# Two splits of 600 rows as 352 and 248, another table for block 0, and an expert's row numbers made tile by tile

## The chip, the cores and the metric
The program runs on one core of one Trainium2 chip. The metric is the device time of one execution in microseconds (us); a kernel's time is the median of several executions. TensorE (PE) does the matmuls and, beside them, the weight loads (PEld); VectorE (DVE) and ScalarE (ACT) do the elementwise work; GpSimd (POOL) issues the indirect transfers (gathers and scatters); SyncE (SP) issues the other transfers.

## The reference
A chunked attention feeds a dense layer pair with a hard-swish, and that feeds a mixture of eight experts with two chosen for each row. Cut to what is computed:

```python
# attention: q, k, v (4, 8, 576, 64), chunks of 64 rows, each chunk for itself
scores = q_c @ k_c.T / sqrt(64); attn = softmax(scores); x = (attn @ v_c)     # -> x (2304, 512)
# dense pair, w_in (512, 2048), w_out (2048, 512)
h = x @ w_in
x = (h * clip(h + 3, 0, 6) / 6) @ w_out
# experts: E = 8, w1 (8, 512, 1024), w2 (8, 1024, 512)
noisy = x @ w_gate + log1p(exp(x @ w_noise)) * noise
top2, top2_w = two largest of noisy per row, softmax over the two
for e in range(8):
    rows = those that chose e
    out[rows] += top2_w * (relu(x[rows] @ w1[e]) @ w2[e])
```

## The kernel before
**Precision.** Each float32 operand is split in a high and a low part, and a product is three matmul passes (high x high, high x low, low x high; `PASSES`). Weights come from memory as `raw` (SyncE, L165), ScalarE makes the high part (L171) and VectorE the low part (L172).

**Dense pair.** The 2304 rows go in five blocks of 4, 3, 4, 4 and 3 tiles of 128 rows. A unit is 128 of the 2048 inner columns: the first layer (`s1`, L346) gives a bank that ScalarE and VectorE turn into `g`, and the second layer (`s2`, L358) adds it to a sum per row tile. Block 0 runs beside the attention and beside the unpacking of the weights. Its order on TensorE, VectorE and ScalarE is written out by hand in the strings `FIRST` and `REST`: `s3.1` is unit 3's first layer, pass 1 (L391), `y3.1` its second layer (L416), `rl`, `rm`, `g`, `gl` the four steps from the one to the other (L397 to L409), `ca`, `cb`, `ct`, `wh`, `wl` the unpacking of a unit's weights (L194 to L220), `sc` to `xo` the steps of an attention tile. Blocks 1 to 4 follow.

**Routing.** The gate of a block is laid among the matmuls of the next work by `route`, in ticks: `tick()` is called after every three matmuls of `s2` and runs what is due. `gate_pos` (two small matmuls, L600 and L601) turns the choice into a place in each expert's list, a scatter writes row number and weight to a table in memory (L623), and `exp_slots` reads a part of that table back (SyncE, L634).

**Experts.** `groups` holds, in order, expert 0 in two parts of three and two tiles, experts 1 to 6 whole (five tiles, `CT`; 600 rows at most, `CAP`), and expert 7 in two parts. Each has eight units `u` of 128 inner columns. For a whole expert a unit begins with two first-layer parts of 300 columns each, 24 matmuls in all; its second layer is written transposed, each weight block with 352 (L741) and 248 (L745) columns. A group in parts has as many columns in a first-layer matmul as it has rows.

Experts 0 and 1 fetch their rows by one gather for a tile (`exp_gather`, L676), and TensorE transposes them. From expert 2 on, a tile is fetched as quarter rows by four gathers of 128 quarter rows (`exp_gather_q`, L659; the last tile has three), whose numbers `iq` VectorE makes from the row numbers `tq` (`exp_index`, L653). `tq` comes by one load from the table and three copies (SyncE, L645, L647). VectorE turns the quarters (`exp_tr_q`, L472), ScalarE and VectorE write the high and the low part (L671, L672). A fetched tile lies in one of three buffers (tag `x2`); `iq` and `tq` have one each.

What an expert's rows need is laid in the units of the groups before by `at(side, unit, function, ...)`. In the order of time: `gi == 1` is the second part of expert 0, `gi == 2` is expert 1, from about 527 to 588 us. TensorE, VectorE, ScalarE and SyncE run in the order in which the code is written; GpSimd's order is the scheduler's.

**The end.** In the last unit of the last group, `exp_last` adds the last three units to the two sums tile by tile (L721); `exp_y` scales each sum by the rows' weights and GpSimd scatter-adds it to the output (L799). The second tile's first half is scaled by VectorE (L790), its second half by ScalarE (L791).

Of the kernel before, what the change touches and what calls it, by code (L numbers as in the profile page):

```python
# [19 lines left out]
P = 128  # L20
# [17 lines left out]
def cols(t0, nt, cap=WIDE):  # L38
    return min(cap - t0 * P, nt * P)
# [10 lines left out]
sc0 warm7.4 mx0 sub0 e0 su0 sc1 ra0 mx1 rb0 sc2 nmx1 nm0 e1.0 mx2 pt0 sc3 e1.1 sub2 warm14.2 mx3 e2 ra1 nmx3  # L50
rb1 e3.1 nm1 su2 pt1 warm13.2 e3.0 ca0 ra2 cb0 at1 rb2 ct0 at0 xo1 ra3 nm2 wh0 xo0 rb3 ca2 pt2 hi0 nm3 at2
wl0 pt3 hi1 xo2 lo0 at3 s0.0.0 lo1 hi2 xo3 cb2 s0.1.0 hi3 lo2 s0.2.0 ct2 s0.0.1 lo3 wh2 s0.1.1 ca1 s0.2.1
wl2
# [3 lines left out]
ca6 wh3 rm1 s2.2 wl3 g1 cb6 y1.0 rl2 gl1 ct6 y1.1 rm2 wh6 y1.2 ca5 g2 wl6 sc4 ca8 cb5 s3.0 mx4 ct5 s3.1 nmx4  # L57
gl2 wh5 s3.2 e4.0 cb8 y2.0 wl5 e4.1 ca7 y2.1 ct8 ca10 wh8 y2.2 cb7 ra4 ct7 s4.0 cb10 wh7 s4.1 rl3 rb4 wl8
rm3 s4.2 wl7 g3 rl4 ca9 y3.0 gl3 ct10 y3.1 cb9 wh10 y3.2 rm4 wl10 g4 s5.0 nm4 s5.1 ct9 gl4 wh9 pt4 ca12 s5.2
at4 wl9 cb12 y4.0 ca11 ct12 y4.1 cb11 wh12 y4.2 ct11 wl12 wh11 xo4 rl5 wl11 sc5 hi4 rm5 s6.0 mx5 g5 lo4 s6.1  # L60
nmx5 gl5 e5.0 s6.2 ca14 cb14 y5.0 e5.1 ca13 ct14 y5.1 ra5 cb13 wh14 y5.2 rb5 ct13 s7.0 wl14 wh13 ca16 s7.1
rl6 cb16 rm6 s7.2 ct16 g6 rl7 y6.0 gl6 wh16 wl13 y6.1 wl16 rm7 y6.2 ca15 g7 s8.0 cb15 ca18 s8.1 ct15 gl7
wh15 s8.2 cb18 y7.0 ca17 wl15 y7.1 ct18 cb17 wh18 y7.2 ct17 s9.0 wl18 wh17 nm5 s9.1 wl17 pt5 ca20 rl8 s9.2
at5 rm8 cb20 g8 rl9 y8.0 gl8 ca19 y8.1 ct20 cb19 wh20 y8.2 ca22 ct19 xo5 cb22 wh19 sc6 hi5 wl20 s10.0 mx6
wl19 s10.1 nmx6 ct22 e6.1 s10.2 rm9 lo5 g9 wh22 ca21 y9.0 gl9 rl10 cb21 e6.0 y9.1 wl22 y9.2 ct21 rm10 wh21
s11.0 g10 wl21 s11.1 gl10 ca24 s11.2 ra6 cb24 y10.0 ca23 ct24 y10.1 cb23 wh24 ct23 y10.2 wl24 wh23 s12.0
ca26 wl23 s12.1 rl11 cb26 rm11 s12.2 ct26 g11 rl12 rb6 y11.0 gl11 wh26 ca25 y11.1 wl26 cb25 y11.2 ca28 ct25
s13.0 nm6 wh25 s13.1 rm12 wl25 g12 pt6 gl12 s13.2 at6 ca27 cb28 y12.0 ct28 y12.1 cb27 wh28 y12.2 ct27 wl28
wh27 xo6 wl27 s14.0 rl13 ca30 hi6 cb30 s14.1 rm13 ct30 s14.2 g13 lo6 wh30 y13.0 gl13 wl30 y13.1 rl14 ca29
y13.2 cb29 ct29 s15.0 rm14 wh29 s15.1 g14 wl29 gl14 s15.2 ca31 y14.0 cb31 ct31 y14.1 rl15 wh31 rm15 y14.2  # L70
wl31 g15 gl15
"""
EARLY = 384
# [7 lines left out]
def tile_kernel(ctx, tc, qkv, w1u, w2u, wg, noise, out):  # L81
# [269 lines left out]
    def s2(acc, g, w, tiles, first, last, passes=None):  # L351
# [32 lines left out]
    def first_s1(u, i, half=None):  # L384
        w, n = st["w", "m", u], BT[0] * P
        if ("h0", u) not in st:
            st["h0", u] = hbank(n) if u else pairs[0][:, :n]
        a, b = (((0, 0), (0, 1), (1, 0)) if u else ((0, 0), (1, 0), (0, 1)))[i]
        c = slice(0, n) if u else slice(half * n // 2, (half + 1) * n // 2)
        for kd in range(KD):  # L390
            nc.tensor.matmul(st["h0", u][:, c], w[:, a, kd * P:(kd + 1) * P], xb[0][:, b, kd, c],  # L391
                             start=(i == 0 and kd == 0), stop=(i == 2 and kd == KD - 1))

    def first_rl(u):
        h, r = st["h0", u], work.tile([P, DM], F32, tag="r", bufs=2, name="r")
        st["r0", u] = r
        nc.scalar.activation(r, h, AF.Relu, bias=b3)  # L397

    def first_rm(u):
        h, r = st["h0", u], st["r0", u]  # L400
        nc.vector.scalar_tensor_tensor(r, r, 6.0, h, op0=ALU.min, op1=ALU.mult)
# [855 lines left out]
```

## Time and profile before

| | |
|---|---|
| time, median of 3 executions | 925.06 us (924.91, 925.06, 928.58) |
| the profiled execution: its own time, and its span | 928.22 us, 926.3 us |
| mean granted clock of TensorE | 0.991 of full |
| TensorE busy | 902.0 us, 97% of the span |
| VectorE, ScalarE, GpSimd busy | 53%, 35%, 25% |

The profile is of one execution; its time stands a little above its span, which is the stretch that the records cover. Busy times are sums over the span. A matmul's end is modelled, so that the spacing of starts, or a row of the chain that ended last, tells more of its cost than its own length.

### The profile page before, as it was taken

What the parts mean: (1) busy time and instruction counts of PE and PEld (TensorE: products, weight loads), DVE (VectorE), ACT (ScalarE), POOL (GpSimd) and SP (SyncE); (2) the same over time, 40 slices, a digit from 0 to 9 for tenths busy, and PEclk for the clock granted to TensorE, in tenths of its full rate; (3) what the DMA queues carried; (4) which work ended last, traced back from release to release, by engine and by line L of the source; (5) the groups of instructions that cost most, each with busy time, mean ns of one, the idle gap of its engine ahead of it and who ended that gap; (6) DMA issues with size and microseconds to landing.
All of it is one profiled execution on the core that took longest, in us unless ns stands there. A gap on an engine that the chain in (4) does not pass through costs nothing.

```text
span 926.3 us, 15379 instructions
## 1 busy us (share of the span) xinstructions
PE 902.0 (97%) x6271; PEld 800.0 (86%) x6271; DVE 495.4 (53%) x950; ACT 321.7 (35%) x611; POOL 230.5 (25%) x212
## 2 busy tenths in 40 slices
PE   8999999999999999999999989899999999999996
PEld 5777788877788777888988889899999999999985
DVE  7999956535543553356542624454655565462321
ACT  5555433323332332245532512142342424332110
POOL 0000000030002000204015172448273645605051
PEclk9999999999999999999999998999999999999999
DMA  9736522122247400035433741277776848654462
GB/s 341 241 106 196 165 75 86 49 61 63 69 170 258 130 13 1 1 101 129 147 104 70 190 119 44 52 208 183 187 159 150 204 121 229 155 154 74 109 80 33
DMA packets 68993, 116.38 MB, mean 126 GB/s; under 512 B 17936, under 2 KB 38544, under 8 KB 68912
## 3 DMA queue, kind: packets, MB, share of 16 engines
q1 hardware_dynamic: 57552, 95.33, 33.8%
q0 software_dynamic: 11360, 19.98, 11.8%
q8 instruction: 51, 0.84, 0.4%
q14 instruction: 30, 0.25, 0.1%
HBM read 85.13 MB, written 30.09 MB: 124 GB/s over the span
## 4 chain that ended last, share of the span: by engine, by line
PE 88%; DVE 6%; DMA 2%; issue 1%; ACT 1%; POOL 0%; POOLq 0%; SPq 0%; ACTq 0%
PE bp L346 40%; PE bp L358 22%; PE bp L741 10%; PE bp L745 7%; PE bp L416 2%; DVE u L199 1%; PE bp L391 1%; DVE u L204 1%; PE pair L314 1%; DMA raw<-in_w1u_dram 1%; DVE w L220 1%; PE pair L232 1%; PE pair L293 1%; DMA lead<-in_qkv_dram 1%; DVE u L194 1%
## 5 line engine op out<-in xcount | busy, mean ns | idle before, releaser
L358 PE MATMUL bp<-w,g 128*128 128x512 f32 (+1 forms) x906 | 231.0, 398 | 0.1
L346 PE MATMUL bp<-Xa,w 128*128 128x300 f32 (+3 forms) x1152 | 195.0, 320 | 3.1 <-issue 2.8
L358 PEld LDWEIGHTS bp<-w,g 128*128 128x128 f32 (+1 forms) x906 | 165.6, 187 | 35.4 <-DVE g L435 1.0
L346 PEld LDWEIGHTS bp<-Xa,w 128*128 128x128 f32 x1152 | 173.3, 190 | 16.0 <-issue 6.1
L741 PE MATMUL bp<-g,w 128*128 128x352 f32 x576 | 162.2, 324 | 3.9 <-issue 3.9
L745 PE MATMUL bp<-g,w 128*128 128x248 f32 x564 | 155.7, 278 | 1.2 <-issue 1.2
L713 DVE SCALAR_TENSOR_TENSOR g<-bp,g 128x300 fp32r<-128x300 f32 (+2 forms) x127 | 59.2, 469 | 175.8 <-ACT g L712 119.8
L623 POOL DMA_INDIRECT table<-pay,slot x36 | 36.0, 1001 | 439.6 <-DVE slot L620 430.2
L659 POOL DMA_INDIRECT xrq<-x2d,iq x114 | 117.9, 1034 | 106.2 <-DVE arena L472 61.2
L712 ACT ACTIVATE g<-bp 128x300 fp32r<-128x300 f32 (+2 forms) x127 | 53.4, 421 | 241.4 <-PE bp L346 188.2
L745 PEld LDWEIGHTS bp<-g,w 128*128 128x128 f32 x564 | 106.4, 189 | 5.1 <-issue 4.6
L741 PEld LDWEIGHTS bp<-g,w 128*128 128x128 f32 x576 | 108.6, 189 | 1.1 <-issue 1.1
L346 PE MATMUL bp<-Xb,w 128*128 128x384 f32 (+1 forms) x480 | 105.7, 363 | 0.0
L346 PE MATMUL bp<-Xe,w 128*128 128x300 f32 (+1 forms) x672 | 104.2, 311 | 0.1
L346 PEld LDWEIGHTS bp<-Xe,w 128*128 128x128 f32 x672 | 99.3, 193 | 1.2 <-issue 0.4
L346 PEld LDWEIGHTS bp<-Xb,w 128*128 128x128 f32 x480 | 85.7, 188 | 11.1 <-issue 0.9
L799 POOL DMA_INDIRECT out_dram<-arena,tab x40 | 64.5, 1612 | 118.3 <-ACT arena L779 72.9
L172 DVE TENSOR_TENSOR w<-raw,w 128x1024 fp32r<-128x1024 f32 x64 | 78.2, 1222 | 28.9 <-ACT w L171 22.7
L423 DVE SCALAR_TENSOR_TENSOR r<-r,bp 128x384 f32<-128x384 f32 (+1 forms) x64 | 39.7, 620 | 82.0 <-ACT r L422 76.4
L422 ACT ACTIVATE r<-bp,b 128x384 f32<-128x384 f32 (+1 forms) x64 | 40.4, 632 | 106.0 <-PE bp L346 104.8
L171 ACT ACTIVATE w<-raw 128x1024 fp32r<-128x1024 f32 x64 | 67.2, 1050 | 5.5 <-PE bp L358 5.2
L435 DVE TENSOR_TENSOR g<-r,g 128x384 fp32r<-128x384 f32 (+1 forms) x64 | 40.0, 625 | 40.1 <-ACT g L427 38.8
(179 smaller groups left out, 796.9 us busy)
## 6 DMA issues: line engine op xcount, KB each, us to landing
raw<-in_w2u_dram SPq DMA_DIRECT2D x64, 512.0 KB
raw<-in_w1u_dram SPq DMA_DIRECT2D x24, 512.0 KB
arena<-in_qkv_dram SPq DMA_DIRECT2D x14, 768.0 KB
turned<-arena SPq DMA_DIRECT2D x24, 304.0 KB
out_dram<-zero SPq DMA_DIRECT2D x4, 1536.0 KB
yr<-turned SPq DMA_DIRECT2D x6, 1024.0 KB
rawx<-in_w1u_dram SPq DMA_DIRECT2D x8, 512.0 KB
x2d<-x SPq DMA_DIRECT2D x15, 256.0 KB
```

Of the source, the lines that this page charges most:

```text
L171: nc.scalar.activation(w[:, 0], raw, AF.Copy)
L172: nc.vector.tensor_tensor(w[:, 1], raw, w[:, 0].bitcast(F32), op=ALU.subtract)
L346: nc.tensor.matmul(dst, w[:, a, kd * P:(kd + 1) * P], x[:, b, kd, t0:t0 + n], start=(k == 0), stop=(k == 3 * KD - 1))
L358: nc.tensor.matmul(acc[i][:gi.shape[2]], gi[:, a], w[:, b, DM:], start=(first and j == 0), stop=(last and j == 2))
L422: nc.scalar.activation(r, st["h", b], AF.Relu, bias=b3)
L435: nc.vector.tensor_tensor(g[:, 1], st["r", b], g[:, 0].bitcast(F32), op=ALU.subtract)
L659: nc.gpsimd.indirect_dma_start(out=xr[:, c * P:(c + 1) * P], out_offset=None, in_=x2q, in_offset=bass.IndirectOffsetOnAxis(ap=st["iq", key ...
L712: nc.scalar.activation(hi[:, t0:t0 + n], h, AF.Relu)
L713: nc.vector.scalar_tensor_tensor(lo[:, t0:t0 + n], h, 0.0, hi[:, t0:t0 + n].bitcast(F32), op0=ALU.max, op1=ALU.subtract)
L741: nc.tensor.matmul(acc[c][:, :BIG], wc, g[a][:, :BIG], start=first, stop=last)
L745: nc.tensor.matmul(small[:, off:off + CAP - BIG], wc, g[a][:, BIG:CAP], start=False, stop=last and off > 0)
L799: s = nc.gpsimd.indirect_dma_start(out=out, out_offset=bass.IndirectOffsetOnAxis(ap=tab[:n, i, 0:1], axis=0), in_=y, in_offset=None, compu ...
```

## The change
- `EARLY` is 352 where it was 384: the two parts of experts 0 and 7 have 352 and 248 rows (before 384 and 216), and functions that took a tile number take a row number.
- `FIRST` and `REST`, the tables of block 0, are written anew; the same steps stand in another order. Attention tile 0's output and unit 0's first layer use other banks, and a small table of the set-up lies elsewhere (not shown).
- `exp_index` makes the row numbers of a range of tiles. Expert 2's list is read in unit 1 of the second part of expert 0 (before in unit 4), the row numbers and the gathers of its tile 0 stand in unit 5 there, those of the others in the units of expert 1 from unit 1 on, and its transposes in units 3 to 7 of expert 1. Expert 3's list is read in unit 3 of expert 1 (before unit 1).
- The gate of the last but one block ends two ticks later (24 becomes 26), what follows it one tick later.
- The last group sums its second tile in two banks of 256 columns, and VectorE scales both.

```diff
-def cols(t0, nt, cap=WIDE):
-    return min(cap - t0 * P, nt * P)
+def cols(r0, nt, cap=WIDE):
+    return min(cap - r0, EARLY if nt == 3 else nt * P)
...
 REST = """
-s1.0 rl0 cb1 rm0 s1.1 ct1 g0 s1.2 ca4 wh1 gl0 y0.0 wl1 cb4 y0.1 ca3 ct4 y0.2 cb3 wh4 rl1 s2.0 wl4 ct3 s2.1
+s1.0 rl0 ca4 rm0 s1.1 ct1 g0 s1.2 cb4 wh1 gl0 y0.0 rl1 wl1 y0.1 rm1 ct4 g1 y0.2 ca3 wh4 cb3 s2.0 wl4 s2.1
...
-EARLY = 384
+EARLY = 352
...
-            nc.tensor.matmul(acc[i][:gi.shape[2]], gi[:, a], w[:, b, DM:],
-                             start=(first and j == 0), stop=(last and j == 2))
+            for y, c in (acc[i] if isinstance(acc[i], list) else [(acc[i], 0)]):
+                nc.tensor.matmul(y[:gi.shape[2]], gi[:, a], w[:, b, DM + c:DM + c + y.shape[1]],
+                                 start=(first and j == 0), stop=(last and j == 2))
...
-    def exp_index(key):
-        tq = st.pop(("tq", key))
-        iq = work.tile([P, CT * KD], I32, tag="iq", bufs=1, name="iq")
-        nc.vector.tensor_scalar(iq[:, :tq.shape[1]], tq, float(KD), quarter, op0=ALU.mult, op1=ALU.add)
-        st["iq", key] = iq
+    def exp_index(key, i0=0, i1=CT):
+        tq = st["tq", key]
+        if i0 == 0:
+            st["iq", key] = work.tile([P, CT * KD], I32, tag="iq", bufs=1, name="iq")
+        c = slice(i0 * KD, min(i1 * KD, tq.shape[1]))
+        nc.vector.tensor_scalar(st["iq", key][:, c], tq[:, c], float(KD), quarter, op0=ALU.mult, op1=ALU.add)
...
-        for i in range(nt):
+        first, halves = st["acc", key]
+        for i, y, c in [(0, first, 0)] + [(1, *y) for y in halves]:
...
+            if key == (NE - 1, 1):
+                st["acc", key] = [bank("p5", [P, DM], "acc"),
+                                  [(bank(f"p{6 + i}", [P, DM // 2], "acc"), i * DM // 2) for i in range(2)]]
...
-            if (key, i) == ((NE - 1, 1), nt - 1):
-                nc.vector.tensor_scalar(y[:, :DM // 2], acc[:, :DM // 2], sc, None, op0=ALU.mult)
-                nc.scalar.activation(y[:, DM // 2:], acc[:, DM // 2:], AF.Copy, scale=sc)
+            if isinstance(acc, list):
+                for half, c in acc:
+                    nc.vector.tensor_scalar(y[:, c:c + DM // 2], half[:n], sc, None, op0=ALU.mult)
...
-    at(side, 0, route, len(GRP) - 2, groups[0], NROW - BT[NB - 1] * P, 24, 3, 18)
+    at(side, 0, route, len(GRP) - 2, groups[0], NROW - BT[NB - 1] * P, 26, 3, 17)
...
-            at(side, 4, exp_slots_q, *after)
+            at(side, 1, exp_slots_q, *after)
+            at(side, 5, exp_index, after[0], 0, 1)
+            at(side, 5, exp_gather_q, after[0], 0)
         elif gi == 2:
-            at(side, 0, exp_index, nxt_[0])
             for i in range(nxt_[3]):
-                if i > 2:
-                    at(side, i, exp_tr_q, nxt_[0], i - 2)
-                at(side, i, exp_gather_q, nxt_[0], i)
-                if i == 1:
-                    at(side, 2, exp_tr_q, nxt_[0], 0)
-            at(side, 5, exp_tr_q, nxt_[0], 3)
-            at(side, 6, exp_tr_q, nxt_[0], 4)
-            at(side, 1, exp_slots_q, *after)
+                at(side, 3 + i, exp_tr_q, nxt_[0], i)
+                if 0 < i < 3:
+                    at(side, i, exp_index, nxt_[0], i, (2, nxt_[3])[i - 1])
+                if i > 0:
+                    at(side, i, exp_gather_q, nxt_[0], i)
+            at(side, 3, exp_slots_q, *after)
             at(side, 5, exp_index, after[0])
```

On VectorE, before, at the first units of expert 1 (buffer numbers are kept, since `g` then tells the units apart; `bp3` and `bp4` are the two parts of a unit's first layer):

```order
L793 TENSOR_SCALAR arena_96<-bp0_464,tab_4426 128x512
L653 TENSOR_SCALAR iq_4871<-tq_4725,quarter_88 128x20
L172 TENSOR_TENSOR w_4878<-raw_4765,w_4878 128x1024
L713 SCALAR_TENSOR_TENSOR g_4883<-bp3_466,g_4883 128x300
L713 SCALAR_TENSOR_TENSOR g_4883<-bp4_467,g_4883 128x300
```

And now, from the same place on, the three units that follow:

```order
L801 TENSOR_SCALAR arena_96<-bp0_464,tab_4425 128x512
L172 TENSOR_TENSOR w_4877<-raw_4771,w_4877 128x1024
L717 SCALAR_TENSOR_TENSOR g_4882<-bp3_466,g_4882 128x300
L717 SCALAR_TENSOR_TENSOR g_4882<-bp4_467,g_4882 128x300
L658 TENSOR_SCALAR iq_4761<-tq_4628,quarter_88 128x4
L717 SCALAR_TENSOR_TENSOR g_4941<-bp3_466,g_4941 128x300
L717 SCALAR_TENSOR_TENSOR g_4941<-bp4_467,g_4941 128x300
L658 TENSOR_SCALAR iq_4761<-tq_4628,quarter_88 128x12
L172 TENSOR_TENSOR w_5000<-raw_4803,w_5000 128x1024
L717 SCALAR_TENSOR_TENSOR g_5005<-bp3_466,g_5005 128x300
L717 SCALAR_TENSOR_TENSOR g_5005<-bp4_467,g_5005 128x300
L475 STREAM_TRANSPOSE arena_96<-xrq_4763 128x512
```

The one instruction that made 20 columns of row numbers (five tiles) is three: 4 columns in expert 0's second part, ahead of these rows, then 4, then 12, each after the lower half of a later unit.

On SyncE, before, from the load of expert 1's list on (`tab` is a list with weights, `tq` the row numbers for quarter rows, `raw` weights):

```order
L634 DMA tab<-table 128x2x2
L634 DMA tab<-table 128x5x2
L165 DMA raw<-in_w2u_dram 128x1024 x3
L634 DMA tab<-table 128x5x2
L645 DMA tq<-table 32x20x1
L647 DMA tq<-tq 32x20 x3
L165 DMA raw<-in_w2u_dram 128x1024 x5
```

And now:

```order
L639 DMA tab<-table 128x2x2
L639 DMA tab<-table 128x5x2 x2
L648 DMA tq<-table 32x20x1
L650 DMA tq<-tq 32x20 x3
L165 DMA raw<-in_w2u_dram 128x1024 x9
```

The loads of expert 2's list and row numbers stand ahead of three weight loads that stood ahead of them, and expert 3's stand behind nine weight loads in a row.

On TensorE, before, at the end of expert 7's second part (`gl` is the last unit's `g`):

```order
L346 MATMUL bp_467<-Xa,w 128x216 x12
L721 MATMUL bp_464<-w,g 128x512 x6
L721 MATMUL bp_464<-w,gl 128x512 x3
L721 MATMUL bp_465<-w,g 88x512 x6
L721 MATMUL bp_465<-w,gl 88x512 x3
```

And now:

```order
L346 MATMUL bp_467<-Xa,w 128x248 x12
L726 MATMUL bp_463<-w,g 128x512 x6
L726 MATMUL bp_463<-w,gl 128x512 x3
L726 MATMUL bp_3602<-w,g 120x256 x6
L726 MATMUL bp_3602<-w,gl 120x256 x3
L726 MATMUL bp_3603<-w,g 120x256 x6
L726 MATMUL bp_3603<-w,gl 120x256 x3
```

The second tile's nine matmuls of 512 columns are two times nine of 256, one half after the other.

## Rows read from the trace of the kernel before

**Rows 1.** The page's first part: busy time, share of the span, instructions.
```profile
PE 902.0 (97%) x6271; PEld 800.0 (86%) x6271; DVE 495.4 (53%) x950; ACT 321.7 (35%) x611; POOL 230.5 (25%) x212
```

**Rows 2.** Windows of 20 us: length, busy PE, PEld, DVE, ACT, POOL, then PEclk.
```profile
60.00:80.00 20.00, 19.14 (x143) 14.88 (x141) 19.59 (x36) 9.00 (x15) 0.00 (x0) 1.00 0.47 153
80.00:100.00 20.00, 18.84 (x79) 14.54 (x80) 18.98 (x37) 10.23 (x29) 0.00 (x0) 1.00 0.64 203
...
540.00:560.00 20.00, 15.19 (x94) 14.42 (x93) 4.62 (x7) 3.27 (x6) 13.37 (x13) 0.85 0.31 81
...
580.00:600.00 20.00, 17.38 (x111) 16.27 (x110) 6.54 (x13) 3.83 (x7) 8.41 (x8) 0.91 0.22 57
```

**Rows 3.** The chain that ended last, 505 to 720: start us, us, what.
```profile
532.17 3.30 PE bp L346 x24
...
545.61 3.30 PE bp L346 x24
...
559.21 5.54 PE bp L346 x22
568.05 3.30 PE bp L346 x24
...
599.52 3.30 PE bp L346 x24
...
652.59 3.30 PE bp L346 x24
...
705.99 3.30 PE bp L346 x24
```

**Rows 4.** GpSimd's timeline: start us, us, what, idle before and its releaser.
```profile
541.96 1.00 POOL L659 DMA_INDIRECT xrq<-x2d,iq  x1 [0.30 <-issue]
...
556.10 0.94 POOL L659 DMA_INDIRECT xrq<-x2d,iq  x1 [0.30 <-issue]
...
575.24 0.94 POOL L659 DMA_INDIRECT xrq<-x2d,iq  x1 [10.34 <-DVE iq L653]
...
589.83 0.95 POOL L659 DMA_INDIRECT xrq<-x2d,iq  x1 [0.31 <-issue]
...
689.64 1.02 POOL L659 DMA_INDIRECT xrq<-x2d,iq  x1 [0.30 <-issue]
...
698.52 0.94 POOL L659 DMA_INDIRECT xrq<-x2d,iq  x1 [0.30 <-issue]
```

**Rows 5.** ScalarE's timeline in the two stretches.
```profile
555.73 0.42 ACT L712 ACTIVATE g<-bp 128x300 fp32r<-128x300 f32 x1 [9.49 <-remote]
...
592.12 0.42 ACT L712 ACTIVATE g<-bp 128x300 fp32r<-128x300 f32 x1 [6.27 <-remote]
```

**Rows 6.** Transfers from 545 to 560: the instruction queue's packets, MB, share.
```profile
q8 instruction: 1, 0.02, 0.4%
```

**Rows 7.** The chain that ended last, 868 to 926 (expert 7).
```profile
876.68 2.09 PE bp L346 x12
878.77 2.10 PE bp L358 x9
...
907.81 1.33 PE bp L346 x12
```

**Rows 8.** VectorE's timeline: the low part of expert 2's tile 4.
```profile
580.28 0.56 DVE L672 TENSOR_TENSOR Xa<-arena,Xa 128x384 fp32r<-128x384 f32 x1 [0.59 <-ACT Xa L671]
```

**Rows 9.** SyncE's waits, 485 to 530: us in total, times, longest us.
```profile
SPq L165 <- DVE g L713: 27.0, 4, 18.8
```

**Rows 10.** TensorE's timeline around the position matmuls of the last but one gate.
```profile
413.24 2.64 PE L358 MATMUL bp<-w,g 128*128 128x512 f32 x9
...
416.37 2.36 PE L346 MATMUL bp<-Xa,w 128*128 128x384 f32 x12
```

**Rows 11.** Timelines of ScalarE and GpSimd at the end.
```profile
917.93 0.47 ACT L791 ACTIVATE arena<-bp,tab 88x256 f32<-88x256 f32 x1 [4.33 <-DVE arena L790]
...
918.70 1.58 POOL L799 DMA_INDIRECT out_dram<-arena,tab  x1 [0.77 <-ACT arena L791]
```

More of the change, by code (lines that the diff above doesn't have):

```diff
@@ L72 @@
+y13.2 lo6 rm14 s15.0 ca31 g14 cb31 s15.1 ct29 s15.2 gl14 wh29 ct31 y14.0 rl15 wl29 wh31 y14.1 rm15 wl31 g15
+y14.2 gl15
 """
-EARLY = 384
+EARLY = 352
 RB = 21
@@ L390, in first_s1 @@
         for kd in range(KD):
-            nc.tensor.matmul(st["h0", u][:, c], w[:, a, kd * P:(kd + 1) * P], xb[0][:, b, kd, c],
+            nc.tensor.matmul(st["h0", u][:, c] if u else st["h0", 0][:, half], w[:, a, kd * P:(kd + 1) * P], xb[0][:, b, kd, c],
                              start=(i == 0 and kd == 0), stop=(i == 2 and kd == KD - 1))
@@ L396, in first_rl @@
         st["r0", u] = r
-        nc.scalar.activation(r, h, AF.Relu, bias=b3)
+        nc.scalar.activation(r if u else r.rearrange("p (a n) -> p a n", a=2), h, AF.Relu, bias=b3)
     def first_rm(u):
         h, r = st["h0", u], st["r0", u]
+        if u == 0:
+            r = r.rearrange("p (a n) -> p a n", a=2)
         nc.vector.scalar_tensor_tensor(r, r, 6.0, h, op0=ALU.min, op1=ALU.mult)
@@ L628, in gate_ps, with exp_slots, exp_slots_q @@
                 st["tab_st"].append(s)
-    def exp_slots(key, e, t0, nt, off):
+    def exp_slots(key, e, r0, nt, off):
         tab = work.tile([P, CT, 2], I32, tag="tab", bufs=10, name="tab")
-        r0 = e * RGN + t0 * P
+        st["xg", key] = xview(off, cols(r0, nt))
+        st["n", key] = cols(r0, nt, CAP)
+        r0 += e * RGN
         nc.sync.dma_start(tab[:, :nt], table[r0:r0 + nt * P, :].rearrange("(t p) c -> p t c", p=P))
         st["tab", key] = tab
-        st["xg", key] = xview(off, cols(t0, nt))
-        st["n", key] = cols(t0, nt, CAP)
-    def exp_slots_q(key, e, t0, nt, off):
-        exp_slots(key, e, t0, nt, off)
+    def exp_slots_q(key, e, r0, nt, off):
+        exp_slots(key, e, r0, nt, off)
         tq = work.tile([P, CT * KD], I32, tag="tq", bufs=1, name="tq")
-        r0 = e * RGN + t0 * P
+        r0 += e * RGN
         tq = tq[:, :nt * KD]
@@ L720, in exp_last @@
                 for j, (a, b) in enumerate(PASSES):
-                    nc.tensor.matmul(st["acc", key][i][:g.shape[2]], g[:, a], w[:, b, DM:],
+                    nc.tensor.matmul(y[:g.shape[2]], g[:, a], w[:, b, DM + c:DM + c + y.shape[1]],
                                      start=False, stop=(u == U2 - 1 and j == 2))
@@ L892, in table_init @@
         nc.gpsimd.iota(pay[:, :, :, 0], pattern=[[P, NTILE], [0, 2]], base=ND, channel_multiplier=1)
-        tmpi = work.tile([P, NE * RB, 2], I32, tag="r", bufs=2, name="tmpi")
+        tmpi = arena[:, 6, :2 * NE * RB].bitcast(I32).rearrange("p (j c) -> p j c", c=2)
         pm = work.tile([P, 2], I32, tag="tab", bufs=10, name="pm")
@@ L943, in step @@
         elif name == "xo":
[L944 removed]
+            att_xo(t, *pair)
         else:
@@ L1119, in tile_kernel @@
     prevg = None
-    for gi, (key, e, t0, nt, off) in enumerate(groups):
+    for gi, (key, e, r0, nt, off) in enumerate(groups):
         side = {}
```

51 lines of the change are left out of this document (24 added, 27 removed).

## The prediction

> **What bounds the kernel now.** I read the page's busy table first: TensorE is busy for 902.0 of 926.3 us, VectorE and ScalarE for 53% and 35% [rows 1]. So a change can gain in only two ways: it takes columns off TensorE, or it removes one of the few places where TensorE waits. The sum of those places is about 24 us. I looked for them in 20-us windows [rows 2]. The poorest between the opening and the tail is 540 to 560 with 15.19 and a granted clock of 0.85, then 580 to 600 with 17.38 at 0.91. The opening shows a milder loss (60 to 100), with VectorE then as full as TensorE.
>
> Next I took the chain that ended last, from 505 to 720. Where an expert has five tiles, a unit begins with 24 matmuls of 300 columns that take 3.30 us, so the starts of those rows are a clock for the units. Eight units take 53.07 us from 599.52 to 652.59, and 53.40 from there to 705.99, but 67.35 from 532.17 to 599.52 [rows 3]. Expert 1, with the start of expert 2, thus loses 67.35 - 53.07 = 14.28 us. Two stalls make it up. From 545.61 to 568.05 two units take 22.44 instead of 2 x 6.60 = 13.20: 9.24 lost. The rest, 5.04, is lost between 568.05 and 599.52. In the first stall the 22 matmuls at 559.21 take 5.54, at the lower of the clock's two levels, where 22/24 of 3.30 is 3.03: 2.5 of the 9.24 is clock, granted low after TensorE had paused.
>
> What goes on beside the stalls? GpSimd's timeline [rows 4] shows twelve gathers of quarter rows one behind the other, 0.94 us each with 0.30 between them, from 541.96 to 557.04, and again from 575.24 to 590.78. These are the only two runs of twelve, and each stall lies in the second half of one. ScalarE is late there too: it stood idle for 9.49 us before its relu at 555.73, and 6.27 before that at 592.12, each time released by something that the records don't name [rows 5]. Later experts gather in runs of four, three and once eight (689.64 to 699.46), and lose next to nothing: the eight units with that run took 0.33 more than the eight before. Why a long run holds the other engines the rows do not say. Instruction fetch is the obvious suspect, but its queue moved one packet in 545 to 560 [rows 6].
>
> **The change, part by part.** The sum is made against the profiled execution, 928.22 us with a span of 926.3.
>
> *A, row numbers and gathers.* Before, the index for all of expert 2 stands at the head of expert 1, the gathers of tiles 0 to 2 are free to run at once, and those of tiles 3 and 4 as fast as transposes free one of three buffers. Now tile 0's index and gather lie in the last unit but two before expert 1, tile i's gather in unit i, its transposes in unit 3 + i. Expert 3's first three gathers keep their units, but each now waits for a buffer that a transpose of units 5, 6 or 7 frees. No more than four gathers then stand in one unit of 6.60 us, which is the pattern of the experts that run at 53.4. I take that pace, not 53.07: 67.35 - 53.40 = 13.95 gained. Bounds: 14.28 if nothing is lost, 9.24 if only the first run is broken up (below).
> What is late next? Tile 4's transposes move from expert 1's unit 6 to unit 7. Before, the last piece for TensorE ended at 580.28 + 0.56 [rows 8]; unit 6 began at 568.05 + 6.60 = 574.65, so it took 6.2 us. In unit 7 that is 0.4 before expert 2 begins, and the columns of tile 4 are read only in the second half of expert 2's first 24 matmuls, 1.65 later: 2.0 us of margin. The loads of expert 2's list and row numbers go to SyncE's queue three units earlier. There they stand ahead of weight loads that wait 18.8 us for VectorE anyway [rows 9], so they cost nothing as long as they end inside that wait; where they stand before, the weight loads behind them have no such wait. VectorE makes expert 2's row numbers in three instructions, of 4, 4 and 12 columns, where it made one of 20, and it is busy for 53% [rows 1]: nothing.
>
> *B, 352 and 248 rows for 384 and 216.* In expert 7's first part 12 matmuls of 384 columns take 2.10 us, 175 ns each; in its second part 12 of 216 take 1.33, 111 ns each [rows 7]. With 300 columns it is 3.30/24 = 137.5 [rows 3]. From 384 to 300 a column costs 0.45 ns, so 352 costs 160.5 by this slope, 14.6 ns less; over 12 matmuls 0.175 us. From 300 down to 216 the slope is 0.32: 248 lies at 123 by that line, and at 111 to 114 if 216 stands on a floor. For the floor speaks that TensorE runs as many weight loads as matmuls [rows 1], and these do not get shorter with fewer rows. I take 114, 3 ns more, 0.035 us a unit; the other end is 12 ns, 0.145. Sixteen units of each kind (experts 0 and 7): 16 x 0.175 = 2.8 less 0.56 is 2.2 gained; bounds 0.5 and 2.8. Second layers keep their 512-column matmuls, 2.10 for nine [rows 7]; the two halves of 256 that expert 7's last tile uses in place of one 512 have the same columns, at 117 ns each still above the 111 of 216.
> The Trainium skill, "TensorE: Matmul & The Clock Gate", section "Back-to-back issue gap", has the gap of an isolated matmul linear in its columns (N/2.4 + 2.5 ns when warm). By it 352 + 248 costs just what 384 + 216 does, B would be 0 and the sum 2.2 us smaller. The rows above are not linear (0.45 ns a column at the long end, less at the short), so the measurement decides, and it gives B.
>
> *C, the end.* Before, ScalarE's half of the last tile stands behind VectorE's (0.47 us after it), and the scatter leaves GpSimd after both, at 918.70 [rows 11]. After, TensorE finishes half 0 nine matmuls of 256 columns, 1.05 us (half of the 2.10 of nine with 512), before half 1, and VectorE evicts it under those matmuls; what remains behind the last matmul is one eviction of about 0.47. I take -0.5; bounds 0 and -0.7. The last part has 120 rows instead of 88 in the scatter: I price it at nothing, since its 1.58 is the time in which GpSimd issues it, and the bounds of C hold the rest.
>
> *D, gate ticks.* At 413.24 nine matmuls that take 2.10 elsewhere [rows 7] last 3.13 until the next group at 416.37 [rows 10], because the two small position matmuls wait for VectorE's counts. Two ticks (six matmuls) later they no longer wait: -0.9; bounds 0 and -1.0. Expert 0's slots and gathers come one tick, 0.7 us, later; the units that lie between them and their transposes hide that, and without such cover it would eat most of the 0.9, which is D's lower bound.
>
> *E, block 0's tables.* The work is the same and only its order changes. TensorE's loss in 60 to 100 is 0.86 + 1.16 = 2.0 us [rows 2], and VectorE is within 0.41 and 1.02 of full in the same windows, so an order can only mend part. I take -0.8; bounds -2.0 and +1.2 (one more wait like that of 80 to 100).
>
> Sum: 13.95 + 2.2 + 0.5 + 0.9 + 0.8 = 18.35. The profiled execution would come to 909.9. The median of the runs shown lies 3.2 lower, at 925.06, with one run at 928.58. That gap is about what the low clock cost in the first stall (2.5 of rows 3), so either the faster runs had less of a stall to lose (then they end near 909.9) or they are faster all along (906.7). Halfway, I forecast 908. The bounds of the terms give 904 to 912.
>
> **The rivals.**
> *Only the first run is broken up.* Expert 3's first gathers are the same twelve instructions in the same three units; if the index or the buffers come so that they still run as one, the second stall stays. Against it: each buffer is now freed by a transpose one unit after the other. Time: 908 + 5.0 = 913. Chance 0.12.
> *The gathers are not the cause.* The long runs and the stalls may have a common cause, or the stall may come from instruction fetch, and expert 1 keeps its 67.35. For it: the records name no releaser. Against it: two of two long runs have a stall and no short one has. Then B to E alone are left, 4.4: about 922 by the same halfway rule, within the bound below. Chance 0.08. The Trainium skill, "Runtime: NRT & Kernel Launch", section "Instruction fetch mechanics", says that the sequencer fetches blocks through a DMA queue of its own, mostly hidden; the one packet of rows 6 agrees that little is fetched there.
> *Slower.* A gather lands later than the transposes that were written for it, three units behind. VectorE runs in order, so the relus of the unit stand behind that transpose, TensorE pauses and its clock falls, as at 559.21. Each unit then pays 2.5 for the clock and a pause, at least the 0.56 of rows 8: 3.06. In all eight units of expert 1 that is 24.5: 53.07 + 24.5 = 77.6 for 67.35 now, 10.2 more, less the 4.4 of B to E: 5.8 slower, about 931. It decides from a gather that is two units (13 us) late. Against it: four gathers of 1.25 us are issued in 5. Chance 0.04.
>
> **How the numbers follow.** A difference of 0.5%, 4.6 us, is about what a measurement of this kernel can tell from none. The forecast holds 0.73, the three rivals 0.12, 0.08 and 0.04, and 0.03 is for an order in the opening that stalls by more than E's bound. Faster by over 0.5% (below 920.4): forecast and first rival and part of the rest, 0.87. Within it: the second rival, 0.08. Slower: 0.05. The range takes in the terms' bounds, the first rival and what the median's place leaves open: 902 to 914.
>
> **What would show it.** A right: eight units from expert 1's second first-layer group take 53 to 54 us, no half clock between 500 and 620, gathers in runs of at most four to a unit. Wrong: the units still take over 60. B: 12 matmuls of 352 take 1.92 and 12 of 248 1.33 to 1.5. C: no ScalarE eviction behind the last matmul, and 0.5 us less from there to the last scatter. D: nine matmuls at the position matmuls in 2.2. E: the windows from 60 to 100 above 19.5. The prediction is wrong if a new stall appears at expert 2's first unit (a transpose late by more than 2.0 us), or if the opening's VectorE is slower in its new order.

## The result, and the profile after

The changed kernel takes 911.66 us (median of 5, 911.02 to 912.64). The kernel before, run again beside it, takes 926.45 (median of 5, 924.91 to 928.58). The ratio is 0.9835, 95% interval 0.9821 to 0.985: 1.65% faster. The forecast was 908 with a range of 902 to 914. The profiled execution fell from 928.22 to 911.34, by 16.9, where the prediction's sum was 18.35.

The page's first part, then four of the 20-us windows, columns as in [rows 1, 2]:

```profile
PE 892.3 (98%) x6295; PEld 794.0 (87%) x6295; DVE 495.4 (54%) x953; ACT 320.6 (35%) x610; POOL 230.8 (25%) x212
```
```profile
60.00:80.00 20.00, 18.83 (x141) 14.37 (x139) 19.39 (x37) 11.24 (x31) 0.00 (x0) 1.00 0.48 133
80.00:100.00 20.00, 18.97 (x92) 14.92 (x83) 18.91 (x37) 10.14 (x29) 0.00 (x0) 1.00 0.60 189
...
540.00:560.00 20.00, 20.00 (x148) 20.00 (x147) 8.83 (x14) 5.69 (x10) 11.68 (x12) 1.00 0.30 68
580.00:600.00 20.00, 20.00 (x145) 19.91 (x144) 12.11 (x18) 6.64 (x11) 7.99 (x9) 1.00 0.64 170
```

The two poor windows of [rows 2] are full now, at the upper clock; the opening's are no fuller than they were. The chain that ended last, in the stretch of [rows 3]:

```profile
530.57 3.31 PE bp L346 x24
...
570.71 5.09 another core or an unknown queue
...
584.24 3.30 PE bp L346 x24
...
637.31 3.30 PE bp L346 x24
...
690.37 3.30 PE bp L346 x24
```

Eight units from 530.57 take 53.67 us, where they took 67.35; the next two times eight take 53.07 and 53.06. That is 13.7 of the 16.9. A rest of 0.6 is left, and one row says where: from 570.71 the chain waits 5.09 us for something unnamed, which is ScalarE standing idle, as in [rows 5]. GpSimd's timeline there, and ScalarE's, columns as in [rows 4, 5]:

```profile
564.42 0.95 POOL L663 DMA_INDIRECT xrq<-x2d,iq  x1 [4.81 <-DVE iq L658]
...
573.18 0.95 POOL L663 DMA_INDIRECT xrq<-x2d,iq  x1 [0.30 <-issue]
```
```profile
575.88 0.73 ACT L716 ACTIVATE g<-bp 128x300 fp32r<-128x300 f32 x2 [5.17 <-remote]
```

A run of eight gathers is left, from 564.42 to 574.13, and the relu that was late runs 1.7 us after its end. The prediction had written "no more than four gathers" to a unit; the eight are the first four of expert 3 and the next four, which started as soon as a buffer was free. Runs of eight by themselves were nothing new: the prediction read [rows 4] as having one (689.64 to 699.46), but before, experts 2 to 5 have one each, also the expert with 53.07 (637.95 to 648.69). Now three more follow (from 619.58, 674.28 and 727.32), and nothing is lost beside them.

At the end of the span, VectorE, then GpSimd, as in [rows 11]:

```profile
900.38 0.48 DVE L799 TENSOR_SCALAR arena<-bp,tab 120x256 f32<-120x256 f32 x1 [0.57 <-PE bp L726]
```
```profile
899.30 1.57 POOL L807 DMA_INDIRECT out_dram<-arena,tab  x1 [14.80 <-DVE arena L801]
901.17 1.62 POOL L807 DMA_INDIRECT out_dram<-arena,tab  x1 [0.30 <-DVE arena L799]
```

The last scatter starts 0.31 us after VectorE's second half ends (900.86), which is when GpSimd has issued the scatter before it (900.87). From its issue to the span's end (909.6) it is 8.43 us, where it was 926.3 - 918.70 = 7.60.

### The profile page after: what moved, and what is told of

The parts are those of the page before. It is cut to its first block, busy times and chain, and to the rows that moved or that the text cites. A ratio compares the mean times of both kernels' runs of the same rounds, so it can differ in the third digit from the quotient of the medians.

```text
span 909.6 us, 15438 instructions
## 1 busy us (share of the span) xinstructions
PE 892.3 (98%) x6295; PEld 794.0 (87%) x6295; DVE 495.4 (54%) x953; ACT 320.6 (35%) x610; POOL 230.8 (25%) x212
## 4 chain that ended last, share of the span: by engine, by line
PE 88%; DVE 5%; DMA 2%; ACT 2%; POOL 1%; issue 1%; another core or an unknown queue 1%; SPq 0%; POOLq 0%; ACTq 0%; DVEq 0%
PE bp L346 38%; PE bp L359 21%; PE bp L749 10%; PE bp L753 7%; PE bp L419 4%; PE bp L392 3%; PE pair L314 1%; PE pair L232 1%; POOL table L626 1%; PE pair L293 1%; DMA lead<-in_qkv_dram 1%; DMA table<-pay,slot 1%; DVE u L204 1%; PE bp L690 1%
## 5 line engine op out<-in xcount | busy, mean ns | idle before, releaser
L359 PE MATMUL bp<-w,g 128*128 128x512 f32 (+3 forms) x921 | 230.4, 393 | 0.5 <-ACT g L430 0.4
L359 PEld LDWEIGHTS bp<-w,g 128*128 128x128 f32 (+2 forms) x921 | 166.6, 186 | 35.5 <-DVE g L438 0.9
L346 PE MATMUL bp<-Xb,w 128*128 128x384 f32 (+2 forms) x480 | 104.2, 360 | 0.0
L346 PE MATMUL bp<-Xe,w 128*128 128x300 f32 (+1 forms) x672 | 99.8, 303 | 0.0
L346 PEld LDWEIGHTS bp<-Xe,w 128*128 128x128 f32 x672 | 95.5, 188 | 0.8
L346 PEld LDWEIGHTS bp<-Xb,w 128*128 128x128 f32 x480 | 84.7, 188 | 11.3 <-issue 1.1
```

Source lines behind the costliest of these rows:

```text
L346: nc.tensor.matmul(dst, w[:, a, kd * P:(kd + 1) * P], x[:, b, kd, t0:t0 + n], start=(k == 0), stop=(k == 3 * KD - 1))
L359: nc.tensor.matmul(y[:gi.shape[2]], gi[:, a], w[:, b, DM + c:DM + c + y.shape[1]], start=(first and j == 0), stop=(last and j == 2))
```

## The experiments

The theory for the large part: a run of indirect gathers issued back to back on GpSimd holds TensorE and ScalarE from about the eighth or ninth gather on. Rivals: the lost time was VectorE waiting in its queue for gathers that landed late; or the gain came from the change's other parts. Eight units of an expert without loss are 53.07 us in every run, so each experiment is read from the chain's rows for the same unit of two experts one after the other.

**The gathers' places undone, and alone.** `after_old_gathers` is the changed kernel with the lines on `gi == 1` and `gi == 2` of before; `before_new_gathers` is the kernel before with the new lines and the new `exp_index`, and nothing else.

```diff
-            at(side, 1, exp_slots_q, *after)
-            at(side, 5, exp_index, after[0], 0, 1)
-            at(side, 5, exp_gather_q, after[0], 0)
+            at(side, 4, exp_slots_q, *after)
         elif gi == 2:
+            at(side, 0, exp_index, nxt_[0])
...
```

Expected of the first: 

> The changed kernel with expert 2's row numbers, gathers and transposes put back where they were before (all row numbers at the head of expert 1). Theory (long runs of gathers on GpSimd hold TensorE): the two runs of twelve gathers come back, eight units of expert 1 take 65 to 68 us instead of 53.67, and the time rises by 11 to 14 us, to 923 to 926. Rival (the gain came from the other parts, and expert 1 only looked slow): 911 to 914.

Expected of the second: 

> The kernel before with nothing but the new places of expert 2's and 3's row numbers, gathers and transposes. Theory: eight units of expert 1 take 53.4 to 54, and the time falls from 926.45 by 11 to 14 us, to 912 to 915; no clock record at the lower level between 500 and 620. Rival (it needs the other parts as well): over 920.

Measured: 926.88 us (8 runs) and 917.10 (4 runs), beside 930.96 for the kernel before on that chip. The ratios to before are 0.9952 (0.9932 to 0.9972) with the old gathers and 0.9849 (0.9814 to 0.9885) with the new gathers alone. The chains, first with the old places, then with the new ones in the kernel before:

```profile
530.56 3.31 PE bp L346 x24
...
599.35 3.30 PE bp L346 x24
...
652.71 3.30 PE bp L346 x24
```
```profile
532.71 3.30 PE bp L346 x24
...
586.84 3.30 PE bp L346 x24
...
639.91 3.30 PE bp L346 x24
```

Eight units from expert 1's second take 68.79 with the old places and 54.13 with the new ones, each a little over what was expected; with the new ones the granted clock is full in every 20-us window from 500 to 620. The gathers' part is worth 1.5% by itself and the other parts 0.5%. (The absolute times lie above those expected since this chip ran the kernel before at 930.96.)

**Longer runs of gathers that nobody waits for.** `bursts_by_length` adds gathers of rows that nobody reads. Not in the expectation: sixteen more stand at the end of expert 6.

```diff
+    def burst(key, n, w=P):
+        bi, bd = st["bi"], st["bd"]
+        nc.vector.tensor_copy(bi, st["iq", key][:, :8])
+        for c in range(n):
+            nc.gpsimd.indirect_dma_start(out=bd[c // 4 % 2][:, c % 4 * P:c % 4 * P + w], out_offset=None,
+                in_=x2q[:, :w], in_offset=bass.IndirectOffsetOnAxis(ap=bi[:, c % 8:c % 8 + 1], axis=0))
...
+                if gi > 3:
+                    at(side, 7, burst, after[0], 4 * (gi - 3))
```

Expected: 

> The changed kernel with extra gathers whose result nobody reads: four at the end of expert 3, eight at the end of expert 4, twelve at the end of expert 5, each behind the seven or eight gathers that stand there already. Theory (a run of gathers costs TensorE one pause of 0.6 to 1.6 us for each gather past the seventh or so): the 53.07 us of eight units become 56 to 58 with the run of 12, 60 to 65 with 16, and 62 to 68 with 19. Rival (in expert 1 VectorE waited in its queue for gathers that landed late, and TensorE for VectorE): nobody waits for these gathers, so all three stay within 53.0 to 53.6.

Measured: 950.4 us (one run). The chain:

```profile
637.36 3.30 PE bp L346 x24
...
692.64 3.30 PE bp L346 x24
...
755.40 3.87 PE bp L346 x24
...
822.56 4.34 PE bp L346 x24
```

The eight units take 55.28 with a run of 12, 62.76 with 16 and 67.16 with 19: 2.2, 9.7 and 14.1 lost, to work that nobody reads. The first is a little under what was expected. (Read one unit later, as the runs below are, at 644.20, 699.49, 762.82 and 830.44, the losses are 2.2, 10.3 and 14.6: the first matmuls after a stall, 3.87 and 4.34 us instead of 3.30, then count with it. The expectations below use these. The run of 12 has a gap of 1.11 us after the eighth gather. The sixteen at the end of expert 6 cost 12.7: from 863.46 to the last 24 matmuls at 933.25 it is 69.79, in the changed kernel 893.42 - 836.37 = 57.05.) The rival is out: no engine waits for these gathers' data. The pauses can be laid beside the gathers. Three pieces of the chain named issue, and three of GpSimd's gathers, the tenth to twelfth of the run of 16:

```profile
742.11 0.40 issue
743.32 0.63 issue
744.66 0.76 issue
```
```profile
741.79 0.95 POOL L672 DMA_INDIRECT bd<-x2d,bi  x1 [0.30 <-issue]
743.04 0.94 POOL L672 DMA_INDIRECT bd<-x2d,bi  x1 [0.30 <-issue]
744.29 0.95 POOL L672 DMA_INDIRECT bd<-x2d,bi  x1 [0.31 <-DMA bd<-x2d,bi]
```

Here TensorE pauses once for each gather, 0.3 us after it begins, and longer each time, in the middle of matmuls that wait for nothing that the profile shows. Later in the run the two no longer go in step: nine pauses from 742.11 to 752.50 stand beside the last seven gathers. They add up to 5.65 us; the rest of the 10.3 is matmuls that take longer, at the lower of the clock's two levels (0.50 granted from 747 to 755.4).

**Which property of the run counts.** `bursts_by_kind` puts three other kinds of work where those gathers were: eight gathers of 64 bytes to a row, sixteen fills of a tile, eight gathers of 16 rows.

```diff
+        for c in range(n):
+            nc.gpsimd.memset(bd[0], 0.0)
...
+                if gi == 4:
+                    at(side, 7, burst, after[0], 8, 16)
+                if gi == 5:
+                    at(side, 7, compute, after[0], 16)
+                if gi == 6:
+                    at(side, 7, burst, after[0], 8, P, 16)
```

Expected: 

> The changed kernel with three other kinds of extra work on GpSimd, with a result that nobody reads: eight gathers of 128 rows of 64 bytes (not 512) at the end of expert 3, sixteen fills of 128x512 at the end of expert 4, eight gathers of 16 rows (not 128) of 512 bytes at the end of expert 5, each behind the seven or eight gathers that stand there. If the number of row descriptors in a run is what holds TensorE: 60 to 65 for the eight units with the first, 53.1 with the second and the third. If it is the bytes: 53.1 to 54 with the first. If it is GpSimd's being busy at all: over 55 with the second. If it is the number of gather instructions: over 57 with the third.

Measured: 923.0 us (one run). The chain, then two rows of GpSimd's timeline, the fills and the first gather of 16 rows:

```profile
644.76 3.30 PE bp L346 x24
...
706.65 3.30 PE bp L346 x24
...
759.72 3.30 PE bp L346 x24
...
813.88 3.31 PE bp L346 x24
```
```profile
747.19 9.43 POOL L681 MEMSET bd<- 128x512 f32 x16
...
800.11 1.60 POOL L673 DMA_INDIRECT bd<-x2d,bi  x1 [2.86 <-issue]
```

Gathers of 64 bytes cost 61.89 - 53.07 = 8.8 us, nearly as much as those of 512 (10.3): it is not the bytes. The fills, 9.4 us behind eight gathers, cost nothing (53.07): it is not GpSimd's being busy. The gathers of 16 rows cost 1.1, which spoke for the rows. But the last row above shows that they came 2.86 us after the seven before them; so the run was broken, and two properties had changed at once.

**Fewer rows, without a break.** `bursts_rows` is the same `burst` with gathers of 64 rows, of 32, and sixteen of 16 rows alone:

```diff
+                if gi in (4, 5, 7):
+                    at(side, 7, burst, after[0], *{4: (8, 64), 5: (8, 32), 7: (16, 16)}[gi])
```

Expected: 

> The changed kernel with extra gathers of fewer rows, whose result nobody reads: eight of 64 rows at the end of expert 3, eight of 32 rows at the end of expert 4, each behind the eight that stand there, and sixteen of 16 rows at the end of expert 6, alone. If the rows that are asked for in a run are what counts (eight and four gathers of 128 rows cost 2.2 us, eight and eight cost 10.3): about 2 us for the first (1536 rows in the run), under 1 for the second, none for the third. If the number of gathers counts, or GpSimd's time for them: about 10 for the first and the second, over 10 for the third, as for sixteen of 128 rows.

Measured: 943.76 us (one run). The chain:

```profile
643.44 3.30 PE bp L346 x24
...
707.58 3.30 PE bp L346 x24
...
770.62 3.30 PE bp L346 x24
```

64 rows cost 64.14 - 53.07 = 11.1 us, 32 rows 10.0. Sixteen gathers of 16 rows cost 11.5 (from expert 6's last unit at 856.71 to the last 24 matmuls of the span at 925.23 it is 68.52, in the changed kernel 893.42 - 836.37 = 57.05). My theory of the rows is wrong. In these runs the number of gather instructions that follow each other without a break counts, whatever they move; a break of 2.86 us within fifteen took most of the loss away. That the number alone does not decide shows below, in `after_spread`.

**The same number, paced.** `bursts_paced` lets each gather wait for the one before to land.

```diff
+                out=bd[c % m][:, :P], out_offset=None, in_=x2q,
```

Expected: 

> The changed kernel with the extra gathers again, behind the seven or eight that stand there: eight at the end of expert 3 that all write to one place, so that each waits until the one before has landed; twelve at the end of expert 4 that write to two places in turn, so that each waits for the one before the last. If gathers that are issued faster than they are carried out are what holds the other engines: no loss for the first (53.1 to 53.6 for eight units, against 63.3 with eight at full pace), and less than half of the 14.6 us for the second. If the number of gathers in a row is what counts, however they are spaced: 60 to 65 for the first.

Measured: 935.61 us (one run). Only the start can be read: from 643.04 to 696.58 eight units take 53.54, while four paced gathers follow the run of eight, the first at once, the others 4.0, 2.75 and 6.4 us after one another: 0.5 lost, where four at full pace cost 2.2. After that it is no answer, since the paced gathers ran on into the next expert's, held them up, and a run of many followed that was not planned.

**The small parts, undone one by one.** Each is the changed kernel with one part as before.

```diff
-EARLY = 352
+EARLY = 384
```

Expected: 

> The changed kernel with its parts of 384 and 216 rows again, and nothing else undone. Theory (12 matmuls cost 1.92 us with 352 columns and 1.37 with 248, where 384 and 216 cost 2.10 and 1.33): experts 0 and 7 together take 2.2 us longer. Theory on the end (the last scatter is longer with 120 rows than with 88): from the last matmul to the span's end 8.4 us instead of 9.25, so that the time rises by 1.3 to 1.5 us in all. Rival (a matmul's cost is linear in its columns): experts 0 and 7 take the same, and the time falls by 0.8.

Measured: 912.78 us (4 runs), ratio to before 0.985 (0.9828 to 0.9872). In expert 7, 12 matmuls of 384 columns took 2.10 and 12 of 216 took 1.33 there, where the changed kernel has this in its chain:

```profile
852.17 1.92 PE bp L346 x12
...
882.34 1.36 PE bp L346 x12
```

So each unit of 352 columns saves 0.18 and each of 248 costs 0.03 to 0.05. By the starts of the same matmuls, expert 7 takes 51.93 us with 384 and 216 (843.54 to 895.47) and 50.45 in the changed kernel (842.97 to 893.42); expert 0, from 446 on, is 1.0 longer as well. The rival of equal cost is out. From the start of the last 27 matmuls (898.14) to the span's end (911.4) it is 13.3 us, and 13.5 in the changed kernel; two profiles of the changed kernel differ there by 1.0, so 88 or 120 rows in the last scatter cannot be told apart here. From the last matmul to the end it is 9.0, not the 8.4 of the theory on the end.

`after_old_tail` has the sums in two banks of 512 columns, and the last half scaled by ScalarE. Expected: 

> The changed kernel with the sums of the last part in two banks of 512 columns again and the last tile scaled by VectorE, then ScalarE, and 352 and 248 rows kept. Theory (the halves save 0.5 us before the last scatter, and the 120 rows cost 0.8 behind it): from the last matmul to the span's end 9.7 us (changed kernel 9.25, before 8.92), time 0.3 to 0.6 us longer. Rival (the halves themselves make the end longer): 8.9 us or less, time shorter.

Measured: 910.45 us (4 runs), ratio 0.9825 (0.9803 to 0.9847). GpSimd's two last scatters:

```profile
899.28 1.57 POOL L803 DMA_INDIRECT out_dram<-arena,tab  x1 [14.79 <-DVE arena L797]
901.62 1.62 POOL L803 DMA_INDIRECT out_dram<-arena,tab  x1 [0.77 <-ACT arena L795]
```

The span ends at 909.3. The last scatter is issued 0.45 later than in the changed kernel, and the span ends no later: from the first of the two to the end it is 10.0 here and 10.3 in the changed kernel. Issuing the second sooner gained nothing. From the last matmul (900.29) to the end it is 9.0, between the theory's 9.7 and the 8.9 of the rival.

`after_old_tables` has block 0's order and banks of before. Expected: 

> The changed kernel with block 0's order tables of before, and the banks that go with them. Theory (the new order only mends a part of the waits of a stretch in which VectorE is full): block 1's first matmul at 117.2 us instead of 116.6, time 0.6 us longer, not to be told from none in the timed runs. Rival (the order is worth the 2 us that TensorE loses from 60 to 100): 2 us longer.

Measured: 912.50 us (4 runs), ratio 0.9848 (0.9826 to 0.9871). Block 1's first matmuls, in the kernel before, then in the changed one:

```profile
117.22 2.09 PE bp L346 x12
```
```profile
116.62 2.10 PE bp L346 x12
```

With the old tables they start at 117.02, in `before_new_gathers`, which has them too, at 117.54. The changed tables stand in eleven profiles of this document: 116.24 to 117.30, ten of them by 116.70, the median 116.46. So the new tables start block 1 some 0.8 us sooner (median 117.22 of the three with the old ones), which no single pair of profiles could tell. The time of 912.50 is 2.05 above that of `after_old_tail` on the same chip, but the opening does not show it: the profiles start block 1 at 117.02 and 117.30, and differ from expert 1 to expert 7 (318.06 and 317.04).

**One version further.** `after_spread` makes expert 3's row numbers in three pieces too, so that the run of eight of the changed kernel is gone; `after_spread_old_tail` has the old end as well; `after_again` is the changed kernel, on the same chip.

```diff
-            at(side, 5, exp_index, after[0])
-            for i in range(3):
-                at(side, 5 + i, exp_gather_q, after[0], i)
+            at(side, 5, exp_index, after[0], 0, 1)
+            at(side, 7, exp_index, after[0], 1, 2)
+            for i in range(2):
+                at(side, 5 + 2 * i, exp_gather_q, after[0], i)
...
+            if gi == 3:
+                at(side, 0, exp_index, nxt_[0], 2)
+                at(side, 0, exp_gather_q, nxt_[0], 2)
```

Expected of the changed kernel: 

> The changed kernel once more, beside the next two on the same chip: 911 to 913. Every theory expects eight units of experts 3 to 6 at 53.07 and of expert 1 between 53.1 and 54.

Expected of the spread gathers: 

> The changed kernel with expert 3's row numbers made in three pieces too, so that its first three gathers, which now stand in a run of eight and a run of four at the end of expert 1, come one to a unit. Theory: the last 0.5 to 0.9 us of loss between expert 1 and expert 2 go (from expert 2's first matmul to expert 3's 53.1, now 53.56), time 0.4 to 0.9 us shorter than the changed kernel. Rival (that rest is not from the run of eight): the same time.

Expected with the old end: 

> The last kernel with the sums of the last part in two banks of 512 columns again, ScalarE scaling the last half tile. Theory (both last scatters go through as one stream that begins 2.1 us after the first is issued, so that issuing the second 0.45 us sooner gains nothing, and the halves cost 0.15 us of TensorE): 0.1 to 0.4 us shorter than the kernel with the spread gathers alone, 0.6 to 1.2 shorter than the changed kernel. Rival (the changed end is worth 0.5): 0.3 to 0.5 longer than the kernel with the spread gathers alone.

Measured, five runs each: 911.06 (910.67 to 912.13), 910.19 (909.62 to 911.83) and 910.20 (909.77 to 910.28). The chain of the second:

```profile
529.62 3.31 PE bp L346 x24
...
582.70 3.30 PE bp L346 x24
...
636.02 3.30 PE bp L346 x24
```

Eight units take 53.08: the rest of the loss is gone (53.67 and 53.91 in the two profiles of the changed kernel). The time is 0.9 us shorter, about as forecast and little more than the runs differ. The old end makes no difference: neither its theory nor its rival showed.

The next eight units take 53.32, and they hold a longer run than any in the changed kernel. GpSimd's timeline, its first and last rows:

```profile
584.15 1.68 POOL L663 DMA_INDIRECT xrq<-x2d,iq  x1 [3.38 <-DVE iq L658]
...
598.80 0.95 POOL L663 DMA_INDIRECT xrq<-x2d,iq  x1 [0.30 <-issue]
```

These are eleven gathers with 0.30 or 0.31 between them, and they cost 0.25 us; in `after_spread_old_tail` eleven stand in the same place (584.26 to 600.22) and cost nothing (53.07 from 582.80 to 635.87). So the number in a row does not decide alone. Some of the eleven take 1.2 to 1.75 us each, so that they start 1.46 us apart on the mean (1.50 in the other), where the runs that cost 5 us and more start 1.15 to 1.33 apart. Whether it is this pace, or what else moves at the time, no run here separates.

## Why the prediction was right, and where it was not

**A was right, in place, size and kind.** Expected 13.95, measured 67.35 - 53.67 = 13.68. Where the prediction said that long runs are the cause but that the rows do not say why, the experiments went half of the way: gathers that nobody waits for bring the loss, by their number and not by what they move, unless something else, perhaps a slower pace, keeps it away (`after_spread`). What in the chip holds TensorE stays open. The pace of 53.40 was taken for that of the experts with a run of eight; the expert with 53.07 has such a run too, so the 0.33 is not its price. The first two rivals fall: the second stall went too, but for 0.6, and expert 1 did not keep its 67.35. The rival on the slower side did not show: up to 563.84 the units of expert 1 keep their pace (26.42 us for the four from 537.42). One sentence of A was wrong, "no more than four gathers then stand in one unit": the run of eight stands there, and with ScalarE held by it the 2.0 us of margin for tile 4 were used up (the chain goes through its low part, which ends at 579.11, to matmuls at 579.15). In `after_spread`, where nothing holds ScalarE, the margin is enough and nothing is lost.

**B was right to some tenths.** 352 columns save 15 ns a matmul (forecast 14.6; the slope of its own rows, 37.5 ns over 84 columns, gives 14.3) and 248 cost 3 to 4 (forecast 3): 16 x (0.18 - 0.04) = 2.2. The rule of the Trainium skill, "TensorE: Matmul & The Clock Gate", section "Back-to-back issue gap", that the gap of an isolated matmul is linear in the columns, gave 0 for it. The starts of the matmuls in `after_384` say 2.5 for both experts (1.5 and 1.0). Of that 1.1 to 1.7 are left between its time and the changed kernel's two medians.

**C gave nothing.** The step was "what remains behind the last matmul is one eviction of about 0.47. I take -0.5". The eviction was saved and the scatter issued 0.45 sooner, but the span's end does not follow the last scatter's issue. The sum looked at when the last scatter leaves GpSimd, and took for granted that the end follows it. The chain that ended last, before, says otherwise:

```profile
916.37 1.56 POOL out_dram L799
...
918.44 1.21 POOLq L1166
```

It goes through the scatter before the last and GpSimd's queue, past ScalarE's half. From the issue of that scatter to the span's end it is 9.9 us before and 10.1, 10.0 and 10.0 in the three other kernels with the old end (`before_new_gathers`, `after_old_tail`, `after_spread_old_tail`), and 10.3, 11.3 and 10.3 with the new one (the changed kernel twice, `after_spread`). With the old end the last scatter has 88 rows in the first two kernels (9.9 and 10.1) and 120 in the other two (10.0): the 32 more rows cost nothing there. That the last scatter queues behind the one before it is a reading of this, and no run tested it. From the start of the last tiles' matmuls (896.14 and 913.21) to the end it is 13.5 us after and 13.1 before, where 0.5 was to be gained; that the end is worth nothing shows in the timed runs too (910.19 with the new one, 910.20 with the old).

**D was given back on the spot.** The wait for VectorE's counts is gone, but TensorE then waits for the next group's `g`. The profile of TensorE at the place of [rows 10], before and after:

```profile
416.35 0.18 PE L601 MATMUL bp<-macc,ones 128*128 128x32 bf16 x1 [0.41 <-DVE macc L576]
...
418.57 2.63 PE L358 MATMUL bp<-w,g 128*128 128x512 f32 x9
```
```profile
412.12 2.65 PE L359 MATMUL bp<-w,g 128*128 128x512 f32 x9
...
416.00 0.19 PE L603 MATMUL bp<-m,upper 128*128 128x32 bf16 x1
416.04 0.18 PE L604 MATMUL bp<-macc,ones 128*128 128x32 bf16 x1
...
417.44 1.32 PE L359 MATMUL bp<-w,g 128*128 128x512 f32 x4 [0.43 <-ACT g L430]
```

The position matmuls (L603, L604) run without a wait, and 0.43 us are lost behind them, where 0.41 were lost ahead: from the nine matmuls to the next second layer it is 418.57 - 413.24 = 5.33 us before and 417.44 - 412.12 = 5.32 after. The gate's work on VectorE stands ahead of the pieces that the next second layer needs; moving the one that waits did not make it shorter. The step that failed is "two ticks later they no longer wait: -0.9": it did not ask what is late next, as the prediction did for A. The 0.9 was too large besides: it took the slowness of the nine matmuls ahead for a part of that wait, and they take 2.65 now where they took 2.64 [rows 10].

**E came out at its size, but not where it was looked for.** Forecast 0.8, and by the eleven and three profiles above block 1 starts 0.8 sooner. But the gain was priced on TensorE's loss from 60 to 100, and those windows are no fuller (18.83 and 18.97, where 19.14 and 18.84 were, and over 19.5 was the sign). Where in the opening the 0.8 comes from was not found, so the size is in part luck.

**The sum and the place of the median.** By the starts of the same matmuls in the two profiles the span lost 0.6 up to block 1 (E), nothing from there to 446 (D), 1.0 and 1.4 in experts 0 and 7 (B), 14.1 between them (A, and the 0.3 by which the experts after it came below 53.40), and the end grew by 0.4 (C): 16.7 of the forecast 18.35. C and D fell short by 1.8 together, E by 0.2; A and B came out 0.2 over each. The profiled execution thus came to 911.34 instead of 909.9. The rest of the miss against 908 comes from the step "Halfway, I forecast 908". Of the two readings given there, the runs fit the first, that the faster executions of the kernel before had less of a stall to lose: its runs spread over 3.7 us, those of the changed kernel over 1.6, and the median after lies 0.3 above its profiled execution, where that of before (926.45) lies 1.8 below it. No profile of a faster execution of the kernel before was taken to show it. (The terms' "904 to 912" counts from the median 925.06 and not from halfway; the measured 911.66 lies at its edge.)

## What to carry to other kernels

Look for a unit of work that repeats and use its start times as a clock: the difference of 67.35 to 53.07 found the loss and sized it to 0.3 us, where the busy shares (97% to 98%) told almost nothing. Spread the gathers for later work over the units that lie before their use, one tile to a unit; a burst of them that nobody waits for can still stop the engine that bounds the kernel. And for every wait that an edit removes, name what is late next: where that was done (A) the sum held, where it was not (C, D) the gain was lost close behind.

## What the runs showed of the hardware that was not expected

- Runs of eight indirect gathers of 0.95 us with 0.30 between them cost 0 to 1.1 us. Longer ones stop TensorE again and again for 0.2 to 1.8 us, without any wait that the profile shows: 12 in a row cost 2.2 (with one gap of 1.11) to 9.2 us, 16 cost 10.3, 19 cost 14.6. The first pause came with the tenth or eleventh gather, and once with the seventh (before, at 550.02, where four more gathers and a scatter stand right ahead). With 16, 32 or 64 rows to a gather instead of 128, or 64 bytes to a row instead of 512, it is 8.8 to 11.5 us for sixteen all the same. But eleven that started 1.46 to 1.50 us apart on the mean cost 0 to 0.25.
- Neither sixteen fills on GpSimd (9.4 us) behind eight gathers nor a break of 2.9 us in the run brings it on: 0 and 1.1 us. Scatters of 1.6 us between the gathers of a steady expert do not either: GpSimd was at work without a break from 657.57 to 684.8 in the changed kernel, and that expert took 53.06.
- ScalarE is held as well: 5.17 us in the changed kernel, released 1.7 us after the last of eight gathers, 18.78 with 19 in a row, released 2.9 us after the last (820.27), and 9.49 before, released 1.3 us ahead of the end of the run of twelve [rows 5]. Whether the semaphores, the instructions or something else are held was not tried; the queue of instructions moved one packet in 740 to 755 of `bursts_by_length`, within the stall, and one in 765 to 780, behind it.
